# A gated recurrence and a mixing layer on one core: ordering v by DMA, a new work order, and thirteen unread matmuls

## The chip, the cores and the metric
One core of one Trainium2 chip runs the whole program. It has five engines with queues of their own: TensorE (PE, with its weight loads shown as PEld), VectorE (DVE), ScalarE (ACT), GpSimd (POOL) and SyncE (SP), and sixteen DMA engines that all of them share. The metric is device time in microseconds (us) of one execution.

## The reference
For four batches and eight heads, 768 tokens with 48 channels each, a state of 48 x 48 decays and is added to, token by token. The result, 384 wide, goes through a layer that mixes over tokens and channels.

```python
for t in range(S):
    cur = einsum('bhd,bhe->bhde', u * k[t], v[t])
    y[t] = einsum('bhd,bhde->bhe', r[t], state + cur)
    state = w[:, :, None] * state + einsum('bhd,bhe->bhde', k[t], v[t])
x = y.transpose(0, 2, 1, 3).reshape(B, S, H * D)
theta = x @ w_theta
yy = einsum('ts,bsd->btd', w_tok_r, x * cos(theta)) + einsum('ts,bsd->btd', w_tok_i, x * sin(theta))
u_ = x + yy
out = u_ + maximum(u_ @ w_ch, 0)
```

## The kernel before
The recurrence is computed in chunks of 128 tokens, two chunks at a time. Two chunks are called a *pair* here; there are twelve, numbered 0 to 11, three to a batch. For one pair the steps are these.

- **Loads** (lines 505 and 511, on SP). k, r and v come into a ring of nine buffers (`ld`). r is always loaded *paired*: a partition gets two tokens that follow each other, so that a run in memory is 384 bytes long, and one DMA brings 384 KB. k and v are loaded paired only for the pairs in `TWO` (pairs 0 to 3); for the others one chunk at a time, with runs of 192 bytes and 192 KB in one DMA (line 511).
- **Decays** (line 675, DVE or POOL): k and r times tables of powers of w, giving `Kw` and `Rw` in bf16. **Flips** (line 565): PE transposes them in blocks of 128 x 128 into a PSUM bank; line 576 (ACT) or 574 (DVE) copies the bank out as `KT` and `RT`.
- **Scores** (line 714): KT times RT for each chunk, 128 x 128 per head, masked on DVE into `mAT` (line 720). **PD and diag** (lines 727, 736): KT times RT elementwise, summed with u by small matmuls, copied by ACT as `dg` (line 741), and multiplied with v as `yd` (line 744).
- **Outer** (lines 759 and 773): sums of k times v for the state, kept by small steps (`N`, `T`, `Sb`) on DVE, POOL and ACT. **Outputs** (lines 833, 842): state times RT, and mAT times v (`vb`), then x on DVE (line 850).
- **Theta** (line 865), sine and cosine on ACT (lines 870, 873), and z = x times both on DVE (line 876).

The mixing of a batch needs z of its three pairs. For each of its six output chunks, twelve matmuls of 384 columns (line 896) run over WrT and WiT, then `un` on DVE (903), a transpose by DMA (585) or by PE, three matmuls with W_ch (919), and `fin` on DVE (923), which is stored by SP (929). In all there are 288 mixing matmuls. The weights come in bf16 by eight casting DMAs from POOL (line 524), six of them for the token weights, which PE then flips.

**v.** outer wants v in the order in which k was loaded, and outputs wants it in token order. For a paired load the two differ. The cast `v2` (line 628) keeps the paired order and is read by outer2 (line 773). For token order, `put` (line 639) multiplies v2 by a 0/1 matrix, `place`, that POOL fills at the start (lines 434, 435): two matmuls of 384 columns for each chunk. `put out` (line 647 on ACT, 649 on DVE) copies the bank into `vb`. vb is read by outputs and by yd.

**The order of the work.** Nothing runs in the order in which the code names it. Each step is added to a plan with an engine, an assumed duration, what it reads and writes, and the PSUM banks it needs. `RANK` gives each step its priority and `MOVED` the steps that go to their second engine; both lists were found by a search outside the program. `Plan.order` then plays the plan through with its assumed durations, banks and DMA queues, and emits the instructions in the order in which the plan would start them. So each engine's queue is fixed when the program is built, and an engine does not pass a waiting instruction. Steps with `port` (decays, PD, yd, z and others on DVE and POOL) are kept from running on both engines at once.

**Completion semaphores.** The framework gives the DMAs that SP and ACT issue eight completion semaphores, in turn, in the order in which the program names the DMAs. A DMA that takes a semaphore has a wait in front of it, on its issuing engine, until the DMA that had the semaphore before has landed. In the kernel before, all such DMAs are SP's.

**Start.** `stuff` is filled, and twelve steps `warm` are in the plan with 427 ns each, but emit nothing (`range(0)`). Log w is spread over the partitions by two fp32 matmuls (line 428), and a small flip of w and u follows (line 446), copied on DVE (line 450).

Of the kernel before, what the change touches and what calls it, by code (L numbers as in the profile page):

```python
# [18 lines left out]
BF16 = mybir.dt.bfloat16  # L19
# [15 lines left out]
class Plan:  # L35
# [50 lines left out]
    def order(self):  # L86
# [23 lines left out]
        while times or dma_next < math.inf:  # L110
# [26 lines left out]
            for e in engines:  # L137
# [23 lines left out]
                if t.xfer:  # L161
                    q = int(e == POOL)
                    queues[q].append(t)
                    if len(queues[q]) == 1:
                        todo[q] = t.xfer + ns
                else:
                    t.end = done + LAT[e]
# [17 lines left out]
TWO = (0, 1, 2, 3)  # L185
W_BY_DMA = ()
WARM = 12
# [45 lines left out]
    61, 102, 105, 107, 112, 120, 140, 143, 155, 165, 173, 176, 185, 206, 222, 235, 238, 247,  # L233
    255, 267, 290, 377, 378, 390, 409, 412, 421, 441, 453, 542, 573, 593, 605, 615, 702,
# [18 lines left out]
def kernel(  # L253
# [49 lines left out]
    place = sb.tile([C, 2, 2, C], BF16, name="place")  # L303
# [12 lines left out]
    v2s = ring(len(TWO), [C, H, 2, D], BF16, "v2")  # L316
# [38 lines left out]
    def setup():  # L355
# [15 lines left out]
        def stuff_fill():  # L371
            nc.vector.memset(stuff, 1.0)
            nc.vector.memset(stuff.rearrange("p (a b) -> p a b", b=2)[:, :, 1], -0.5)
        P.add(DVE, 250, stuff_fill, wr=["stuff"], prio=-102)
        for i in range(WARM):
            def warm_up(i=i):
                for _ in range(0):
                    nc.tensor.matmul(bank(("warm", i))[:, :2 * C], stuff[:, :C], stuff,
                                     start=True, stop=True)
            P.add(PE, 427, warm_up, rd=["stuff"], acq=[("warm", i)], prio=-92, name="warm")  # L380

# [51 lines left out]
        def placing():  # L433
            nc.gpsimd.memset(place, 0.0)
            nc.gpsimd.affine_select(
                out=place, in_=place, compare_op=Alu.not_equal, fill=1.0, base=0,
                channel_multiplier=-2, pattern=[[C, 2], [-1, 2], [1, C]])
        P.add(POOL, 1200, placing, wr=["place"], prio=-94)

# [3 lines left out]
        P.add(SP, 800, wu_load, wr=["wu"], prio=-90 + 0.0055, xfer=300)  # L443
# [546 lines left out]
```

## Time and profile before

| | us |
|---|---|
| median of three runs (lowest, highest) | 143.91 (141.71, 144.53) |
| the profiled execution | 140.77 |
| its span, first to last instruction | 139.1 |
| PE busy | 124.2 (89%) |
| DVE busy | 107.8 (77%) |
| ACT busy | 75.8 (55%) |
| POOL busy | 73.5 (53%) |

In the lines of the profile, L896 is line 896 of the kernel. The slices divide the span into forty equal parts, and a digit is the busy share in tenths. Matmuls are pipelined: a busy time counts each from its start to its modelled end, so two that follow each other overlap, and the distance of their starts (the pitch) is the better measure of what one costs. "SPq" is SP's instruction stream with its DMA issues.

### The profile page before, as it was taken

The numbers are of one execution on the slowest core, as the hardware profiler recorded it, in microseconds if no ns is written. First come the engines' busy times: TensorE is split into PE (matmuls) and PEld (weight loads), VectorE is DVE, ScalarE is ACT, GpSimd is POOL, SyncE is SP. The second block draws the span as 40 slices with busy tenths as digits, with TensorE's granted clock in tenths as the row PEclk, the third lists the DMA queues.
The fourth block names the chain that finished last, engine by engine and source line by source line (L and its number), as shares of the span: only waits on it lengthen the run. The fifth ranks groups of instructions, "written<-read, shape, count | busy, mean of one in ns | idle before, by whom it ended". The sixth has DMA issues, their size and how long they took to land.

```text
span 139.1 us, 4098 instructions
## 1 busy us (share of the span) xinstructions
PE 124.2 (89%) x1677; PEld 84.6 (61%) x1677; DVE 107.8 (77%) x200; ACT 75.8 (55%) x142; POOL 73.5 (53%) x60
## 2 busy tenths in 40 slices
PE   2389876999999999999999989999799999999980
PEld 2168655876777666677657657675455665656640
DVE  6189989797897799989799889988689665526381
ACT  7969985899965634789413767339751305000010
POOL 6027989994055594996687899499640000000000
PEclk9999999599999999999999999999999999999996
DMA  2899999999989989999997998999862023255644
GB/s 61 230 323 321 308 222 202 195 244 210 207 174 220 194 169 226 152 209 185 158 223 133 233 255 179 223 147 232 169 232 51 7 57 66 106 167 61 170 176 163
DMA packets 72637, 25.24 MB, mean 182 GB/s; under 512 B 67241, under 2 KB 72618, under 8 KB 72618
## 3 DMA queue, kind: packets, MB, share of 16 engines
q1 hardware_dynamic: 70186, 22.03, 77.2%
q0 software_dynamic: 2432, 2.95, 12.2%
q8 instruction: 13, 0.21, 0.6%
q14 instruction: 6, 0.05, 0.2%
HBM read 20.06 MB, written 4.72 MB: 178 GB/s over the span
## 4 chain that ended last, share of the span: by engine, by line
PE 47%; DMA 16%; POOL 13%; DVE 12%; issue 6%; ACT 3%; SPq 0%; POOLq 0%; DVEq 0%; ACTq 0%
PE bank L896 23%; PE bank L919 7%; DMA fin_all<-in_moe_w_tok_r_dram 6%; PE bank L565 6%; POOL PD L727 5%; DMA ld<-in_k_dram 4%; PE bank L865 4%; POOL Rw L675 3%; DMA uu_all<-uu_all 3%; DVE mAT L720 3%; DMA ld<-in_r_dram 3%; POOL yd L744 2%; POOL Kw L675 2%; DVE fin_all L923 2%; ACT KT L576 1%
## 5 line engine op out<-in xcount | busy, mean ns | idle before, releaser
L896 PE MATMUL bank<-z,WrT 128*128 128x384 bf16 x144 | 46.8, 326 | 0.1
L896 PE MATMUL bank<-z,WiT 128*128 128x384 bf16 x144 | 46.8, 326 | 0.0
L720 DVE TENSOR_TENSOR mAT<-bank,mask 128x512 bf16<-128x512 f32 x48 | 30.9, 681 | 2.1 <-PE bank L714 2.0
L727 POOL TENSOR_TENSOR PD<-RT,KT 128x1024 bf16<-128x1024 bf16 x10 | 21.2, 2123 | 2.2 <-DVE z L876 1.1
L675 POOL TENSOR_TENSOR Kw<-ld,kpow 128x768 bf16<-128x768 f32 x7 | 12.7, 1811 | 16.7 <-DVE z L876 8.5
L870 ACT ACTIVATE trig<-bank,pi 128x384 f16<-128x384 f32 x24 | 13.7, 599 | 12.1 <-issue 4.5
L923 DVE SCALAR_TENSOR_TENSOR fin_all<-bank,uu_all 128x384 f32<-128x384 f32 x24 | 12.9, 553 | 9.1 <-PE bank L919 8.9
L896 PEld LDWEIGHTS <-WrT 128*128 128x128 bf16 x144 | 14.1, 98 | 8.4
L896 PEld LDWEIGHTS <-WiT 128*128 128x128 bf16 x144 | 14.1, 98 | 8.3 <-issue 0.2
L903 DVE TENSOR_TENSOR uu_all<-bank,x 128x384 bf16<-128x384 f32 x24 | 13.1, 552 | 6.0 <-PE bank L896 5.3
L744 POOL TENSOR_TENSOR yd<-dg,vb 128x768 bf16<-128x768 f32 x10 | 14.7, 1472 | 3.1 <-ACT dg L741 1.8
L675 POOL TENSOR_TENSOR Rw<-ld,rpow 128x768 bf16<-128x768 f32 x8 | 14.5, 1813 | 2.3 <-PE bank L565 1.4
L919 PE MATMUL bank<-Wch,uu_all 128*128 128x384 bf16 x72 | 14.3, 326 | 1.3 <-DMA uu_all<-uu_all 0.9
L576 ACT ACTIVATE KT<-bank 128x1024 bf16<-128x1024 bf16 (+1 forms) x11 | 10.8, 981 | 8.5 <-PE bank L565 7.3
L865 PE MATMUL bank<-Wth,xT 128*128 128x384 bf16 x72 | 14.5, 326 | 0.0
L576 ACT ACTIVATE RT<-bank 128x1024 bf16<-128x1024 bf16 (+1 forms) x12 | 11.8, 986 | 3.8 <-PE bank L565 3.8
L850 DVE TENSOR_TENSOR x<-bank,yd 128x384 bf16<-128x384 f32 x24 | 12.4, 548 | 1.7 <-issue 0.9
L876 DVE TENSOR_TENSOR z<-x,trig 128x1536 bf16<-128x1536 bf16 x12 | 12.1, 1009 | 0.8 <-ACT trig L873 0.8
L873 ACT ACTIVATE trig<-bank 128x384 f16<-128x384 f32 x24 | 11.9, 512 | 0.0
L565 PE MATMUL bank<-ident,Rw 128*128 128x128 bf16 x96 | 8.1, 230 | 2.5 <-DVE Rw L675 2.4
L919 PEld LDWEIGHTS <-uu_all 128*128 128x128 bf16 x72 | 6.6, 98 | 5.8 <-DMA uu_all<-uu_all 1.3
L576 ACT ACTIVATE uu_all<-bank 128x384 bf16<-128x384 bf16 x1 | 0.5, 490 | 16.7 <-PE bank L565 16.7
(105 smaller groups left out, 190.5 us busy)
## 6 DMA issues: line engine op xcount, KB each, us to landing
ld<-in_r_dram SPq DMA_DIRECT2D x12, 384.0 KB, 4.8
out_dram<-fin_all SPq DMA_DIRECT2D x11, 384.0 KB, 2.8
ld<-in_k_dram SPq DMA_DIRECT2D x16, 192.0 KB, 4.9
ld<-in_v_dram SPq DMA_DIRECT2D x16, 192.0 KB, 5.6
ld<-in_k_dram SPq DMA_DIRECT2D x4, 384.0 KB, 4.9
ld<-in_v_dram SPq DMA_DIRECT2D x4, 384.0 KB, 5.8
x<-in_moe_w_tok_i_dram POOLq DMA_DIRECT2D x1, 384.0 KB, 6.2
z<-in_moe_w_tok_r_dram POOLq DMA_DIRECT2D x1, 384.0 KB, 7.6
```

The source lines that it names most:

```text
L565: nc.tensor.matmul(bank16(tok)[:, i * C:(i + 1) * C], s, ident, is_transpose=True, start=(i == 0), stop=(i == n - 1))
L576: nc.scalar.activation(dst, src, Act.Copy)
L675: eng.tensor_mul(X[:, :, hs, :D], src[:, :, hs], pw[:, :, hs])
L720: P.add(DVE, dve_ns(HP * C), lambda hi=hi, tk=tk, mAT=mAT: nc.vector.tensor_mul(mAT[:, hi], bank(tk[hi]).rearrange("p (h t) -> p h t", h=H ...
L727: eng.tensor_mul(PD, RT, KT)
L744: eng.tensor_mul(yd.rearrange("p a h d -> p (a h) d"), wide(dg, D), vb.rearrange("p a h d -> p (a h) d"))
L865: nc.tensor.matmul(bank(th)[:, :HD], xT[:, t, dk, :], Wth[:, dk, :], start=(dk == 0), stop=(dk == ND - 1))
L870: P.add(ACT, act_ns(HD, False) + 65 + (1300 if g == 0 and t == 0 else 0), lambda th=th, t=t, trig=trig: nc.scalar.activation(trig[:, t, 0] ...
L896: nc.tensor.matmul(bank(tm)[:, :HD], (WrT, WiT)[ri][:, so, to * C:(to + 1) * C], z[:, so, ri], start=(part == 0 and i == 0), stop=(part == ...
L903: P.add(DVE, dve_ns(HD), lambda tm=tm, t=t, to=to, un=un: nc.vector.tensor_add(un[:, t], bank(tm)[:, :HD], x[:, to]), use=[tm], rd=[("x", ...
L919: nc.tensor.matmul(bank(tf)[:, :HD], uT[:, t, dk, :], Wch[:, dk, :], start=(dk == 0), stop=(dk == ND - 1))
L923: nc.vector.scalar_tensor_tensor(fin[:, t], bank(tf)[:, :HD], 0.0, un[:, t], op0=Alu.max, op1=Alu.add),
```

## The change
Five things change.

1. Put, put out and `place` go. In their place `order` issues four DMAs from ACT's queue for each paired v: for each chunk and each of the two interleaved halves, 64 rows of 768 bytes go from v2 to every second row of vb, from SBUF to SBUF. v2 is laid out so that a row is contiguous, and has four buffers.
2. Pair 4 joins `TWO`: its k and v are loaded paired.
3. Thirteen matmuls of 256 columns are emitted right behind the second spread, into the bank that the plan uses last. Nothing reads them. The empty `warm` steps go, and the flip of w and u now stands behind the spreads.
4. Some assumed durations in the plan change, and an ACT step may have a latency (a negative `xfer`).
5. `RANK` and `MOVED` are new, so that every engine's order is new, and some steps change engine. By count, five more PD are on DVE and five fewer on POOL; DVE has two more decays of k, one fewer of r, and two more casts of vb, and POOL takes two more yd.

```diff
-TWO = (0, 1, 2, 3)
+TWO = (0, 1, 2, 3, 4)
...
-    v2s = ring(len(TWO), [C, H, 2, D], BF16, "v2")
+    NV2 = 4
+    v2s = ring(NV2, [C, 2, H, D], BF16, "v2")
...
-        P.add(PE, 300, wu_flip, rd=["wu", "ident_f"], acq=["wu"], prio=-90)
+        P.add(PE, 300, wu_flip, rd=["wu", "ident_f", ("lw", 1)], acq=["wu"], prio=-90)
...
-                def put(tv=tv, c=c, v2=v2):
+            def order_v(vb=vb, v2=v2):
+                for c in range(2):
                     for j in range(2):
-                        nc.tensor.matmul(bank(tv)[:, :HD], place[:, c, j, :], v2[:, :, j, :],
-                                         start=(j == 0), stop=(j == 1))
...
-                P.add(ACT, act_ns(HD, False), lambda f=put_out: f(nc.scalar), use=[tv],
-                      wr=[kv[c]], prio=base + 10 * pr + 1, name="put out",
-                      alt=(DVE, dve_ns(HD), False, lambda f=put_out: f(nc.vector)))
+                        nc.scalar.dma_start(
+                            out=vb[j::2, c].rearrange("p h d -> p (h d)"),
+                            in_=v2[c * Dp:(c + 1) * Dp, j].rearrange("p h d -> p (h d)"))
+            P.add(ACT, 1100, order_v, rd=[("v2", i2)], wr=kv, prio=base + 10 * pr + 1,
+                  xfer=-2500, name="order")
...
-                P.add(PE, 330, scores, rd=kKT + kRT, wr=[("mAT", mi, hi) for hi in range(2)], acq=tk, prio=pb + 2, mode=1,
+                P.add(PE, 240, scores, rd=kKT + kRT, wr=[("mAT", mi, hi) for hi in range(2)], acq=tk, prio=pb + 2, mode=1,
...
-            ns = (210 if last else 430) if two else (110 if last else 310)
+            ns = (300 if last else 620) if two else (150 if last else 400)
...
+        spreads += t.name == "spread"
+        if t.name == "spread" and spreads == 2:
+            for _ in range(13):
+                nc.tensor.matmul(spare[:, :2 * C], stuff[:, :C], stuff, start=True, stop=True)
```

In the built program the eight-semaphore rule now joins SP's loads and ACT's order DMAs. The four order DMAs of pair 4 follow, on their semaphores, the second v half of pair 5, the first k half of pair 6, the r load of pair 6 and the first v half of pair 6; two of pair 2's follow the k and the r load of pair 3; and SP's loads of pairs 3 to 6 follow order DMAs of pairs 0 to 3 in the same way. Behind pair 4's order DMAs on ACT stand the dg copy of pair 4, KT of pair 5, an Sb and RT of pair 5.

More of the change, by code (lines that the diff above doesn't have):

```diff
@@ L160, in order @@
                 out.append(t)
-                if t.xfer:
+                if t.xfer > 0:
                     q = int(e == POOL)
@@ L166, in order @@
                 else:
-                    t.end = done + LAT[e]
+                    t.end = done + LAT[e] - min(t.xfer, 0.0)
                     for b in t.uses:
@@ L184 @@
 U_BY_DMA = tuple(range(11))
-TWO = (0, 1, 2, 3)
+TWO = (0, 1, 2, 3, 4)
 W_BY_DMA = ()
-WARM = 12
 V_CAST = ()
@@ L191 @@
 RANK = [
[38 rows of a table removed]
[37 rows of a table added]
 ]
 MOVED = [
-    61, 102, 105, 107, 112, 120, 140, 143, 155, 165, 173, 176, 185, 206, 222, 235, 238, 247,
-    255, 267, 290, 377, 378, 390, 409, 412, 421, 441, 453, 542, 573, 593, 605, 615, 702,
+    64, 67, 77, 79, 84, 89, 120, 150, 195, 208, 213, 220, 230, 231, 240, 261, 273, 350, 384,
+    414, 496, 502, 515, 520, 534, 566, 578, 588, 675,
 ]
@@ L302 @@
     gate = sb.tile([1, 1], F32, name="gate")
-    place = sb.tile([C, 2, 2, C], BF16, name="place")
     rpow = sb.tile([C, 2, H, D], F32, name="rpow")
@@ L369, in setup @@
               wr=["warm"], prio=-99)
[L371 to L380, printed above, removed]
         def tok():
@@ L431, in setup @@
                   use=[] if s == 0 else ["lw"], wr=[("lw", s)], prio=-98 + s, name="spread")
[L433 to L438, printed above, removed]
         def wu_load():
@@ L442, in wu_load @@
             nc.sync.dma_start(out=wu[HP:, :, :D], in_=u.rearrange("(a b) d -> a b d", b=2))
-        P.add(SP, 800, wu_load, wr=["wu"], prio=-90 + 0.0055, xfer=300)
+        P.add(SP, 800, wu_load, wr=["wu"], prio=-90 + 0.0055, xfer=900)
         def wu_flip():
@@ L620, in front @@
                 continue
-            i2 = g % len(v2s)
+            i2 = g % NV2
             v2 = v2s[i2]
@@ L625, in cast2 @@
                     "p (h q) -> p h q", h=H)[:, :, :2 * D]
-                dst = v2.rearrange("p h j d -> p h (j d)")
+                src = src.rearrange("p h (j d) -> p j h d", j=2)
+                dst = v2
                 if eng is nc.scalar:
@@ L633, in front @@
                   alt=(POOL, pool_ns(2 * HD) - 200, True, lambda f=cast2: f(nc.gpsimd)))
-            for c in range(2):
-                tv = ("V", g, c)
-                def put(tv=tv, c=c, v2=v2):
+            def order_v(vb=vb, v2=v2):
+                for c in range(2):
                     for j in range(2):
-                        nc.tensor.matmul(bank(tv)[:, :HD], place[:, c, j, :], v2[:, :, j, :],
-                                         start=(j == 0), stop=(j == 1))
-                P.add(PE, 340, put, rd=[("v2", i2), "place"], wr=[kv[c]], acq=[tv],
-                      prio=base + 10 * pr + 1, name="put")
-                def put_out(eng, tv=tv, c=c, vb=vb):
-                    src = bank(tv)[:, :HD].rearrange("p (h d) -> p h d", h=H)
-                    if eng is nc.scalar:
-                        eng.activation(vb[:, c], src, Act.Copy)
-                    else:
-                        eng.tensor_copy(vb[:, c], src)
-                P.add(ACT, act_ns(HD, False), lambda f=put_out: f(nc.scalar), use=[tv],
-                      wr=[kv[c]], prio=base + 10 * pr + 1, name="put out",
-                      alt=(DVE, dve_ns(HD), False, lambda f=put_out: f(nc.vector)))
+                        nc.scalar.dma_start(
[3 more added lines that the diff above has]
+                  xfer=-2500, name="order")
         prev = None
@@ L764, in outer, with outer2 @@
                                     skip_group_check=True)
-            def outer2(ts=ts, Kw=Kw, v2=v2s[g % len(v2s)], sums=sums):
+            def outer2(ts=ts, Kw=Kw, v2=v2s[g % NV2], sums=sums):
                 for i, cs in enumerate(sums):
@@ L774, in outer2 @@
                                     bank(ts)[hi * Dp:(hi + 1) * Dp, o:o + D],
-                                    Kw[:n, j, 2 * hp + hi, :], v2[:n, 2 * hp + hi, j, :],
+                                    Kw[:n, j, 2 * hp + hi, :], v2[:n, j, 2 * hp + hi, :],
                                     start=(i == 0 and hp == 0 and j == 0),
@@ L778, in outer2 @@
                                     skip_group_check=True)
-            ns = (210 if last else 430) if two else (110 if last else 310)
-            P.add(PE, ns, outer2 if two else outer, rd=kK + ([("v2", g % len(v2s))] if two
+            ns = (300 if last else 620) if two else (150 if last else 400)
+            P.add(PE, ns, outer2 if two else outer, rd=kK + ([("v2", g % NV2)] if two
                   else kv), acq=[ts], prio=pb + 2, mode=2, name="outer")
@@ L947 @@
     order = P.order()
+    first = {}
+    for t in order:
+        for b in t.acq:
+            first.setdefault(P.bank_of[b], t.start)
+    spare = bank_t[max(range(P.nbanks), key=lambda i: first.get(i, math.inf))]
+    nc.vector.memset(stuff, 1.0)
+    nc.vector.memset(stuff.rearrange("p (a b) -> p a b", b=2)[:, :, 1], -0.5)
+    spreads = 0
     made, before = nc.cur_bb.bb.instructions, None
```

75 rows, old and new, of the table RANK are left out of this document.

## Prediction
> **What bounds the kernel now.** I read the page's forty slices first, then busy time in windows, then the chain of waits, then SP's timeline.
>
> ```profile
> PE   2389876999999999999999989999799999999980
> ...
> DMA  2899999999989989999997998999862023255644
> ```
>
> ```profile
> 7.65:35.00 27.35, 24.32 (x461) 19.00 (x462) 24.04 (x42) 23.34 (x43) 21.95 (x19) 0.94 1.17 251
> 35.00:70.00 35.00, 34.92 (x524) 24.12 (x523) 30.98 (x51) 22.87 (x42) 21.91 (x13) 1.00 1.11 191
> 70.00:105.00 35.00, 33.08 (x476) 22.12 (x473) 30.83 (x55) 19.42 (x36) 27.32 (x17) 1.00 1.06 202
> ```
>
> The columns are stretch, length, then busy us of PE, weight loads, DVE, ACT, POOL, then granted clock, DMA share, GB/s. From 35 us on PE is never short of work for long, so every us by which PE is stopped there is a us of the span. The DMA engines are busy the whole way to 100 us. Before 35 us several engines are near full together and PE is not the only bound.
>
> The chain of waits, in order of time, shows what releases the first mixing matmuls (L896):
>
> ```profile
> 26.38 8.45 DMA fin_all<-in_moe_w_tok_r_dram
> 34.82 0.05 issue
> 34.87 0.84 PE bank L565 x12
> 35.71 0.97 PE bank L865 x6
> 36.69 0.65 PE bank L896 x4
> ```
>
> From 36.69 to the end of the last L919 (135.4) PE takes 98.7 us. At the pitches of the chain (mixing, theta, chan 0.1625 us a matmul, flips 0.056, scores 0.034, small ones 0.02 to 0.04) the matmuls ordered there sum to 94.6 us; 4.1 us are idle and loss. The tail after it (last evacuation, store, barrier) is 139.1 - 135.4 = 3.7 us.
>
> SP's timeline, with the us an issue took in the second column:
>
> ```profile
> 18.96 6.44 SPq L505 DMA_DIRECT2D ld<-in_r_dram  x1
> 25.49 4.29 SPq L511 DMA_DIRECT2D ld<-in_v_dram  x2
> ...
> 29.87 9.78 SPq L511 DMA_DIRECT2D ld<-in_k_dram  x2
> ...
> 44.89 1.06 SPq L505 DMA_DIRECT2D ld<-in_r_dram  x1
> 46.04 3.50 SPq L511 DMA_DIRECT2D ld<-in_v_dram  x2
> ```
>
> The loads of pairs 4 and 5 crawl while POOL's eight weight casts run (16 to 40 us); the list of DMA issues for 18 to 24 us gives the r load of pair 4 16.4 us to landing. The loads of pair 6 are issued only at 42.87 to 47, and land about 5 us later.
>
> **What goes, at its rows.** The sixteen put matmuls (L639) ran at 326 to 527 ns of latency, but by start times the first four took 0.33 us each and the rest 0.163: 4 x 0.33 + 12 x 0.163 = 3.3 us of PE. All but four lie before 20 us, where PE also idles (3.3 of 5 us busy at 20 to 25 us), so only part of it is worth time. Pair 4 becomes paired: 32 small matmuls for 24, +0.2 us PE. Eight put-outs go: 7 x 0.513 on ACT, 0.55 on DVE. The 0/1 matrix: 1.2 us of POOL at 2.0 to 3.2 us, where POOL next waits 6.3 us for a load: nothing. Two loads of 384 KB replace four of 192 KB, at about 1.15 us each in the queue: -2.3 us of SP and DMA.
>
> **The 13 unread matmuls.** They stand behind the spreads, which end at 4.41 us, and ahead of the flip of w and u. At the half-rate pitch of the early rows (0.33 us for 384 columns, so 0.22 for 256) they take 2.8 us and end at 7.2; PE's first useful flip starts at 7.65. They fit that gap. The flip of w and u moves from 5.0 to about 7.2, and its copy on DVE (L450), now second in DVE's decay work, holds the decay of Rw behind it from 7.03 to about 7.6: cost 0 to 0.6 us, I take 0.5. The gain: PE's pitch was half of the later one from 7.65 to about 11 us, 3.3 us of work at double length, so 0 to 1.6 us, 0.66 of which is in the puts already counted. Nothing in the trace shows an earlier start of the full pitch, so both ends stay; I take 1.0. All of it lies ahead of the first mixing matmul, which the weights decide (below), so in the sum it is hidden; it counts only in rival (a).
> The Trainium skill (TensorE: Matmul & The Clock Gate, Part 1) says that the array starts at half rate and is released after some 3.4 us of sustained activity, on a free-running window. By that rule spreads and unread matmuls together (2.8 to 7.2 us) would release it before or soon after 7.65, and the whole 1.6 us would come. The trace agrees in that 7.65 + 3.4 is where the pitch changes, though the granted-clock row shows 1.00 from the start; no run here shows the rest.
>
> **The order by DMA.** Twenty DMAs of 64 rows x 768 B, issued by ACT. No ACT-issued DMA is in the trace. One issue: below by nothing, above by the 1.15 us of SP's issues into a full queue; nearest are SP's shortest (0.37 to 0.53 us), I take 0.42: 8.4 us of ACT, 5.0 of it (three pairs) before 23 us, where ACT is 90% busy. Landing: between the 2.8 us of the output stores and the 16.4 of the load above; nearest is the SBUF-to-SBUF transpose with 3.1, longer while weights run. The 0.98 MB cost about 3 us of DMA at the 325 GB/s of the early loads, against the 2.3 saved.
>
> **The search.** Counting each form in both instruction orders and pricing it by its row: POOL -11.5 us (five PD at 2.12, two Kw at 1.81 go; two yd, one Rw come), DVE +5.0 (five PD at 0.68, two Kw at 0.95, two vb at 1.58 come; two yd at 1.82 go), ACT -6.9 before its 8.4 of issues. DVE is 88% busy at 35 to 105 us; POOL's relief meets no PE wait above 0.8 us in total. I take 0, with -1.5 to +2.5 for what an order of this kind can do to the 4.1 us of idle above.
> Up to the first mixing matmul the weights still decide: in the new order POOL issues three casts behind pair 0's yd (about 18.5 us) and the next behind pair 1's yd, which needs pair 1's dg; that stands on ACT behind eight order DMAs. ACT's work to there, start to start from its rows: the first v2 cast starts at 9.5, behind two half-size evacuations, and takes 0.75; four issues; two full evacuations, two kpow, w256, dg, two v2 casts and two Sb, 5.25; eight issues; RT, KT and dg, 2.0: 17.5 + 12 x 0.42 = 22.5 us; yd, two cast issues (0.8 each) and the 7 to 8 us of landing give 33 to 34, flips and theta 1.6: first mixing at about 35 (34 to 38). So about 1.7 us ahead of 36.69.
>
> **Where it is lost again.** DMAs of SP and ACT share eight completion semaphores, taken in program order, and a DMA waits until the one eight before has landed. In the new order the four order DMAs of pair 4 wait for pair 5's last v half, pair 6's first k half, **pair 6's r load and pair 6's first v half**: prefetches issued just ahead in the program. Before, SP ran behind: it issued pair 6's r load at 44.89, in program order before the vb cast of pair 4, which ACT did at 43.39. When do they land now? In units of 1.15 us, the program before needed 26 loads to that v half, landing 46.04 + 5.6 = 51.6; now it is 24, so -2.3, + about 2.5 for sixteen order DMAs, and the weights start 1 to 2 us later while SP's pair 4 loads wait for pair 1's order DMAs: 50 to 53; ACT would be there at 42 to 45. I take the last landing as 50.5.
> Queued on ACT behind these waits: the dg copy of pair 4, KT of pair 5, Sb, RT. PE waits for the dg copy: scores take the same PSUM bank. From the first mixing matmul to those scores PE has 40 mixing matmuls 6.5, 40 flips 2.25, 16 scores 0.55, 32 outer 0.7, 8 diag 0.3 = 10.3 us; 84.4 remain behind. So PE stops at 35 + 10.3 = 45.3 to 46 and goes on at 50.5 + 0.42 issue + 0.2 copy = 51.1.
> Sum: 51.1 + 84.4 + 4.1 + 3.7 = **143.3 us span**, before 139.1 (check of the method with before: 36.7 + 94.6 + 4.1 + 3.7 = 139.1). The profiled execution took 140.77, 1.67 more than its span: 145.0, a ratio of 1.030. The median of the runs shown, 143.91, is 2.2% above the profiled execution; on that scale 148.2. I give **146.5**, between the two.
>
> **Rivals.**
> (a) *Faster: the prefetches land before ACT asks.* For: the last loads of a batch are free to go as soon as slots and semaphores are, two loads fewer stand ahead, and a load outside the weights' time lands in 4.8 us. Then nothing stops PE: puts -2.4 (part at 20 us idle is lost already), clock -1.6, first mixing at about 33: 139.1 - 4.0 = 135 span, 136.8, on the median scale 139.8. It decides when the last landing comes before 44 us. Against it: DMA share above 1.0 in every window to 50 us. Chance 0.28.
> (b) *Within 2%.* The landing comes at 44.5 to 49, so ACT's wait eats the early gain: 137 to 141.7, as a time 138.6 to 143.4. Also here: the unread matmuls lift no clock and the order is free. Chance 0.24.
> (c) The forecast, 0.48. Inside it, a worse end: PE idles over 4 us at 46 to 51. After the idle stretch at 19 to 23 us the clock row stood at 0.50 from about 24.5 to 27.7; the same again costs 1.7 us, and landings at 53 another 2.5: 147.5 span, 149 to 152.
>
> Range: from between (a)'s two scales (136.8 and 139.8) to near the upper of (c)'s worse end: 138 to 151.5. A measurement of this kernel tells about 2% from no change (its runs spread over 2%). Faster 0.28, same 0.24, slower 0.48.
>
> **What would show it.** PE's pitch for 128-column flips at 7.5 to 11 us: 0.056 if the clock came. ACT with a gap of 5 us or more at 42 to 51 us, in front of or inside the order DMAs of pair 4, and PE idle at 45 to 51 released by dg. First mixing matmul at 34 to 38. If ACT has no such gap, the step of the landing is wrong and (a) holds; if PE's losses lie after 60 us, the search is to blame, and DVE will be the releaser.

## The result, and the profile after

The changed kernel took 149.18 us (median of four runs, 148.81 to 150.27), the kernel before 142.81 (140.59 to 144.53) on the same chip: a ratio of 1.058 with a 95% interval of 1.046 to 1.070. Two of the four executions of the kernel before (143.91 and 144.53) ran in a slower state that some executions of one and the same kernel show, and the ratio compares the other two (141.71 and 140.59) with the changed kernel's four. It is 5.8% slower, where the forecast's 146.5 us was 1.8% above its 143.91. The profiled execution took 150.27 us, its span is 148.6 (139.1 before). It was the longest of the four: the spans of the other three are 147.1 to 147.6, so that differences of spans below can be up to 1.5 us too large.

The forty slices of the changed kernel, as before:

```profile
PE   2959793995999905999999999999999999999990
...
PEclk9995868579999995699999999999999999999998
...
DMA  3999799999997998998999999996551125251635
```

PE has two holes that the kernel before doesn't have: slice 7 (22.3 to 26.0 us) and, empty, slice 15 (52.0 to 55.7); a lesser one is in slice 10. Behind slices 7 and 15, and at 11 us (slice 4), the granted clock is low.

The chain of waits, in order of time (start, length, what):

```profile
17.20 5.83 DMA vb<-v
23.05 11.45 DMA ld<-in_k_dram
34.52 0.97 DVE Kw L645
35.54 0.97 PE bank L545 x14
...
41.77 2.60 PE bank L866 x16
...
50.22 6.41 DMA ld<-in_v_dram
```

Before, this stretch of the chain ran through a weight load. Now it runs through an order DMA of pair 1, a k load of SP that waited for it, the decay of that k (pair 4), its flips, which PE has ahead of the last weight flips, and so to the first mixing matmul (L866), at 41.6 us in place of 36.5 (by the first start of L896; the row of the chain in the prediction begins one matmul later). Farther on the chain goes through a v load of pair 6, a prefetch that no work needs at 50 us.

What waits for it is seen in ACT's timeline (start, length, engine and line, what; in brackets the idle time ahead and what ended it):

```profile
17.86 4.90 ACTq L618 DMA_DIRECT2D vb<-v  x6
22.86 1.02 ACT L556 ACTIVATE RT<-bank 128x1024 bf16<-128x1024 bf16 x1 [4.74 <-DMA vb<-v]
...
47.49 0.86 ACT L609 ACTIVATE v<-ld 128x768 bf16<-128x768 f32 x1
50.79 6.34 ACTq L618 DMA_DIRECT2D vb<-v  x4
57.26 0.18 ACT L711 ACTIVATE dg<-bank 128x16 f32<-128x16 f32 x1 [8.91 <-DMA vb<-v]
```

ACT has cast v of pair 4 at 48.35, issues the first order DMA at 50.79, the last from 56.66 to 57.13, and only then copies dg. The first two rows explain the hole in slice 7: with eight order DMAs of pairs 1 and 2 issued one behind the other up to 22.8, ACT copies RT at 22.86 and KT at 23.78, and PE waits 2.9 us for that KT. Here is SP's timeline, as shown of before:

```profile
23.05 0.37 SPq L485 DMA_DIRECT2D ld<-in_k_dram  x1
...
29.75 13.19 SPq L491 DMA_DIRECT2D ld<-in_k_dram  x2
43.04 2.13 SPq L485 DMA_DIRECT2D ld<-in_r_dram  x1
...
49.04 1.09 SPq L485 DMA_DIRECT2D ld<-in_r_dram  x1
50.22 3.55 SPq L491 DMA_DIRECT2D ld<-in_v_dram  x2
```

The first v half of pair 6 is issued at 50.22 and lands 6.41 us later, at 56.6: it is the load whose completion semaphore the last order DMA of pair 4 takes, and ACT goes on with that landing. Before, SP issued it at 46.04. SP's own loads wait for order DMAs as well: its three waits for them end at 14.35 and 15.30 (pair 3's k and r, behind pair 0's) and at 23.05 (pair 4's k, behind pair 1's). The waits view of PE, ACT and SP (who waits for whom: us in total, times, longest):

```profile
PE bank L684 <- ACT dg L711: 5.2, 1, 5.2
PE bank L684 <- ACT KT L556: 2.9, 1, 2.9
...
ACT dg L711 <- DMA vb<-v: 8.9, 1, 8.9
...
SPq L485 <- DMA vb<-v: 9.4, 3, 6.1
```

### The profile page after: what moved, and what is told of

Read it like the earlier page. It is cut to its first block, busy times and chain, and to the rows that moved or that the text cites. A ratio compares the mean times of both kernels' runs of the same rounds, so it can differ in the third digit from the quotient of the medians.

```text
span 148.6 us, 4133 instructions
## 1 busy us (share of the span) xinstructions
PE 128.4 (86%) x1682; PEld 88.2 (59%) x1682; DVE 107.3 (72%) x209; ACT 69.2 (47%) x130; POOL 62.2 (42%) x53
## 4 chain that ended last, share of the span: by engine, by line
PE 56%; DMA 16%; ACT 8%; POOL 6%; DVE 4%; issue 4%; ACTq 2%; SPq 1%; POOLq 0%
PE bank L866 27%; DMA ld<-in_k_dram 8%; PE bank L545 6%; PE bank L889 6%; PE bank L835 5%; DMA ld<-in_v_dram 4%; DMA vb<-v 4%; POOL PD L697 3%; PE bank L812 3%; PE bank L684 2%; PE bank L933 2%; ACTq L618 2%; ACT RT L556 1%; ACT KT L556 1%; POOL Kw L645 1%
## 5 line engine op out<-in xcount | busy, mean ns | idle before, releaser
L866 PE MATMUL bank<-z,WrT 128*128 128x384 bf16 x144 | 47.2, 329 | 0.0
L866 PE MATMUL bank<-z,WiT 128*128 128x384 bf16 x144 | 47.2, 329 | 0.0
L714 POOL TENSOR_TENSOR yd<-dg,vb 128x768 bf16<-128x768 f32 x12 | 17.7, 1473 | 21.8 <-ACT RT L556 7.8
L873 DVE TENSOR_TENSOR uu_all<-bank,x 128x384 bf16<-128x384 f32 x24 | 13.2, 552 | 10.6 <-PE bank L866 10.2
L645 POOL TENSOR_TENSOR Rw<-ld,rpow 128x768 bf16<-128x768 f32 x9 | 16.4, 1818 | 7.2 <-DVE Kw L645 4.7
L866 PEld LDWEIGHTS <-WrT 128*128 128x128 bf16 x144 | 14.2, 98 | 8.4 <-issue 0.2
L866 PEld LDWEIGHTS <-WiT 128*128 128x128 bf16 x144 | 14.2, 98 | 8.1 <-issue 0.2
L684 PE MATMUL bank<-RT,KT 64*128 64x128 bf16 x192 | 10.2, 239 | 8.6 <-ACT dg L711 5.2
L556 ACT ACTIVATE KT<-bank 128x1024 bf16<-128x1024 bf16 (+1 forms) x10 | 9.8, 981 | 12.2 <-PE bank L545 11.9
L835 PE MATMUL bank<-Wth,xT 128*128 128x384 bf16 x72 | 15.1, 342 | 0.3 <-ACT xT L556 0.3
L645 POOL TENSOR_TENSOR Kw<-ld,kpow 128x768 bf16<-128x768 f32 x5 | 9.1, 1818 | 15.1 <-DVE uw L456 12.5
L889 PE MATMUL bank<-Wch,uu_all 128*128 128x384 bf16 x72 | 14.8, 326 | 0.1
L684 PEld LDWEIGHTS <-KT 64*128 64x128 bf16 x192 | 6.3, 102 | 12.4 <-issue 8.7
L697 POOL TENSOR_TENSOR PD<-RT,KT 128x1024 bf16<-128x1024 bf16 x5 | 10.6, 2123 | 4.0 <-ACT RT L556 4.0
L645 DVE TENSOR_TENSOR Kw<-ld,kpow 128x768 bf16<-128x768 f32 (+1 forms) x8 | 6.9, 861 | 4.3 <-DMA ld<-in_k_dram 2.5
```

The lines of the kernel that those rows point to most:

```text
L556: nc.scalar.activation(dst, src, Act.Copy)
L645: eng.tensor_mul(X[:, :, hs, :D], src[:, :, hs], pw[:, :, hs])
L684: nc.tensor.matmul(bank(tk[hi])[:, hp * C:(hp + 1) * C], KT[q, hp, c, :], RT[q, hp, c, :], start=(hp == 0), stop=(hp == HP - 1))
L697: eng.tensor_mul(PD, RT, KT)
L714: eng.tensor_mul(yd.rearrange("p a h d -> p (a h) d"), wide(dg, D), vb.rearrange("p a h d -> p (a h) d"))
L835: nc.tensor.matmul(bank(th)[:, :HD], xT[:, t, dk, :], Wth[:, dk, :], start=(dk == 0), stop=(dk == ND - 1))
```

## The experiments

The theory after the result: the time went into two waits for completion semaphores, SP's loads behind the order DMAs of pairs 0 and 1, and ACT's order DMAs of pair 4 behind SP's prefetches. The rivals: the new order of the work itself; the DMA engines being too full for these rows whichever queue issues them; the unread matmuls and the clock.

### Order DMAs replaced by copies

```diff
+                if g in (4,):            # or (0, 1, 2, 3), or TWO
+                    nc.scalar.activation(vb, v2, Act.Copy)
+                    return
                 for c in range(2):
                     for j in range(2):
                         nc.scalar.dma_start(
```

> The changed kernel, with pair 4's four order DMAs replaced by one ACT copy of v2 into vb (0.85 us at the row of the v cast). Left out: the token order of pair 4's v. Theory (PE's stop at 52.2 to 57.5 us is ACT waiting for the semaphores of pair 6's prefetches): dg of pair 4 is there before PE's scores, PE does not stop, first mixing matmul still at 41.6; 41.6 + 10.3 + 84.4 + 2.8 to 4.1 + 3.7 = 142.8 to 144.1 us of span, less up to 1.7 for half-rate matmuls behind the stop: 141 to 144, against 148.6. Rival (the new order of the work is at fault, and the wait only covers it): PE stops near 52 us for DVE or ACT all the same, span 146 to 149.

> The changed kernel, with the order DMAs of pairs 0 to 3 replaced by one ACT copy each; pair 4 keeps its four. Left out: the token order of v in pairs 0 to 3. Theory (SP's loads of pair 4 stand behind the order DMAs' semaphores, and this moves the first mixing matmul from 36.7 to 41.6 us): SP issues pair 4's k load at about 17 instead of 23 us, first mixing matmul at 36 to 38; SP then reaches pair 6's r load at about 45, its v half lands at 51 to 53, so PE stops from 47 to 52: span 143 to 145. Rival (the weights or DVE's extra work set the first mixing matmul): it stays at 40 to 42, span 147 to 149.

> The changed kernel, with all twenty order DMAs replaced by five ACT copies; unread matmuls, the paired pair 4 and the new order of the work stay. Left out: the token order of v in the paired pairs. Theory (all of the loss is in the two waits for DMA semaphores): first mixing matmul at 36 to 38, no stop of PE at dg; 37 + 10.3 + 84.4 + 3.5 + 3.7 = 139, so 137 to 141 us of span, level with the kernel before (139.1). Rival (the new order itself costs several us): over 142.

Measured. copy_pair4: span 143.7, and PE has no stop at dg; the first mixing matmul is at 43.3, so the saving is that of the second wait alone. Its times spread from 142.54 to 147.36, so no size is read from it; pair4_by_pool, below, tests the same wait with times that agree. copy_pairs0to3: span 143.8, ratio 1.027 (1.019 to 1.036), first mixing at 38.3. copy_all: span 138.6, ratio 0.992 (0.989 to 0.996), first mixing at 38.6 and no stop. The spans of the three profiled executions lie in the theories' ranges. The first mixing matmuls do not: 43.3 where 41.6 was expected, 38.3 and 38.6 where it was 36 to 38. In copy_all what follows takes 100.0 us in place of the kernel before's 102.6. So the new order of the work, the paired pair 4 and the unread matmuls, together with the dropped puts, are no loss: all of the loss is in the twenty DMAs. copy_pairs0to3 gains 4.7 us by the medians, all twenty together 9.5.

SP's and ACT's timelines in copy_pairs0to3 show the second wait by itself:

```profile
45.55 2.26 SPq L491 DMA_DIRECT2D ld<-in_v_dram  x2
```

```profile
45.04 6.80 ACTq L621 DMA_DIRECT2D vb<-v  x4
51.96 0.18 ACT L714 ACTIVATE dg<-bank 128x16 f32<-128x16 f32 x1 [6.95 <-DMA vb<-v]
```

SP, no longer held by order DMAs, issues pair 6's v halves from 45.55, the first lands at 51.3, ACT issues the last order DMA at 51.37 and copies dg at 51.96. PE goes on at 52.20.

### The same DMAs with other semaphores

```diff
+                queue = nc.gpsimd if g in (4,) else nc.scalar
                 for c in range(2):
                     for j in range(2):
-                        nc.scalar.dma_start(
+                        queue.dma_start(
```

> The changed kernel with one difference: pair 4's four order DMAs are issued from POOL's queue, whose DMAs have completion semaphores of their own, in place of ACT's. The same bytes are moved between the same buffers at the same place of the work. Theory (PE's stop at 52 us is made by the semaphores that ACT's order DMAs share with SP's prefetches, not by moving v by DMA): ACT copies dg of pair 4 at 47 to 51, PE does not stop for it, span 141 to 145 against 148.6, as with pair 4 copied (143.7). POOL pays four issues of about 0.8 us (the row of the cast issues) ahead of its decays of pair 5. Rival 1 (the DMA engines are too full at 47 to 57 us for these rows, whichever queue issues them): vb of pair 4 lands at 56 or later, PE stops in outputs or yd instead, span 147 to 149. Rival 2 (POOL's issues hold its decays, and PE waits for Kw or Rw of pair 5): 145 to 148.

Measured: 145.17 us against 149.18, span 143.4, ratio 1.031 (1.025 to 1.037). POOL's timeline, and ACT's copy of dg in the same run:

```profile
47.07 2.16 POOL L619 DMA_DIRECT2D vb<-v  x4 [0.23 <-issue]
49.24 1.83 POOL L646 TENSOR_TENSOR Kw<-ld,kpow 128x768 bf16<-128x768 f32 x1
...
54.11 1.87 POOL L715 TENSOR_TENSOR yd<-dg,vb 128x768 bf16<-128x768 f32 x1 [0.82 <-DMA vb<-v]
```

```profile
48.19 0.18 ACT L712 ACTIVATE dg<-bank 128x16 f32<-128x16 f32 x1 [1.41 <-PE bank L707]
```

Four issues took POOL 2.16 us, and nothing held them; dg is copied at 48.19, released by PE and no longer by a DMA. The first is issued at 47.07, and yd, which needs all four, waits for the last of them to 54.1. This run settles the point that the copies could not: the bytes, the buffers and the place in the work are those of the changed kernel, only the queue and with it the semaphores differ, and PE's 5.2 us at dg are gone. That it is the semaphores and not something else in ACT's queue rests on the landings: in the changed kernel ACT's last order DMA starts at 56.66, as that v half lands (56.63), and in copy_pairs0to3 at 51.37, as it lands there; at 10.36, with the DMA engines full as well (share 1.17), ACT issued four in 2.48 us. Rival 1 falls; of rival 2 a little is true (PE waits 1.7 us for Kw from POOL).

The Trainium skill (DMA: Bandwidth & Descriptors, Rules for kernel authors) says that spreading DMAs over SP, ACT and GpSimd doesn't help bandwidth and only saves the sequencers' issue time. Here moving four DMAs saved 4.0 us by the medians, by a third thing: which DMAs an issue must wait for.

### Fewer and larger order DMAs

```diff
-                    for j in range(2):
-                        nc.scalar.dma_start(
-                            out=vb[j::2, c].rearrange("p h d -> p (h d)"),
-                            in_=v2[c * Dp:(c + 1) * Dp, j].rearrange("p h d -> p (h d)"))
+                    nc.scalar.dma_start(out=vb[:, c], in_=v2[c * Dp:(c + 1) * Dp])
```

> The changed kernel with two order DMAs for each pair instead of four (one for each chunk, 64 partitions x 1536 B read, 128 rows of 768 B written): same bytes, half the issues and half the semaphores. Pair 4's two then follow pair 5's first v half and pair 6's first k half; SP's pair 4 loads follow fewer order DMAs. Theory (issues and shared semaphores cost the time, not the bytes): first mixing matmul at 37 to 40, PE's stop at dg 0 to 2 us, span 139 to 144. Rival (the bytes, moved row by row beside the weights, are what is slow): span 146 to 149.

Measured: span 141.9, ratio 1.024 (1.015 to 1.033), first mixing at 38.2, stop at dg 0.6 us. SP waits 1.8 us for order DMAs in place of 9.4 and issues pair 6's first v half at 46.92 in place of 50.22, with the same bytes moved. There are fewer issues, too, so this run alone doesn't part issues from semaphores. PE also waits for vb (0.85) and for a PD that POOL starts late behind a yd that waits for vb (1.4). The list of DMA issues of the changed kernel and of this run (count, KB each, median us to landing):

```profile
vb<-v ACTq DMA_DIRECT2D x20, 48.0 KB, 5.0
```

```profile
vb<-v ACTq DMA_DIRECT2D x10, 96.0 KB, 4.8
```

Twice the bytes land in the same time, and an issue costs ACT about the same 0.62 us (1.23 for two, 2.48 for four in the changed kernel). The Trainium skill (DMA: Bandwidth & Descriptors, Rules for kernel authors) says that below 64 KB one pays mostly overhead. These rows fit that, but loads kept the DMA engines full, and how much of the 5 us was queueing no run shows.

### The order DMAs alone, in the kernel before

```diff
                 def put(tv=tv, c=c, v2=v2):
-                    for j in range(2):
-                        nc.tensor.matmul(bank(tv)[:, :HD], place[:, c, j, :], v2[:, :, j, :],
-                                         start=(j == 0), stop=(j == 1))
+                    return
...
                 def put_out(eng, tv=tv, c=c, vb=vb, v2=v2):
+                    for j in range(2):
+                        nc.scalar.dma_start(
+                            out=vb[j::2, c].rearrange("p h d -> p (h d)"),
+                            in_=v2[c * Dp:(c + 1) * Dp, j].rearrange("p h d -> p (h d)"))
```

> The kernel before with the order DMAs alone: put emits nothing, put out issues two order DMAs from ACT for its chunk, v2 is laid out by rows; pair 4 unpaired, old order of the work, no unread matmuls. Theory (the order DMAs hold ACT and, by their semaphores, SP's loads of pairs 3 and 4, in any order of the work): ACT idle behind order DMAs by 2 to 6 us before 30 us, first mixing at 37.5 to 41, span 139.5 to 144. Rival (only the new order brings DMAs and loads into each other's way): 3.3 us of put matmuls and 4 us of ACT are gained, span 136 to 139.

Measured: span 151.2, ratio 1.083 (1.078 to 1.088), first mixing at 40.5. Worse than the theory's range of spans, by a second stop that it did not count; and the waits of ACT that it expected before 30 us came at 33 to 45. PE's timeline:

```profile
42.18 0.50 PE L840 MATMUL bank<-vb,mAT 128*128 128x48 bf16 x8
48.81 0.48 PE L840 MATMUL bank<-vb,mAT 128*128 128x48 bf16 x8 [6.13 <-DMA vb<-v]
```

Here it is pair 3 whose outputs stop PE: two of its order DMAs are issued at 33.35, the other two only at 43.67, each held on ACT by a load of SP (ACT's idle times of 3.5 and 5.3 us at 37 and 45 us end with a landing of `ld<-in_k_dram`). So the mechanism needs neither the new order nor the paired pair 4; with the order DMAs in it the old order is the slower one (1.083 against 1.058).

### The unread matmuls and the clock

In the changed kernel `range(13)` becomes `range(0)`; in the kernel before, thirteen are emitted behind the second spread as in the changed kernel.

> The changed kernel without the thirteen unread matmuls. In the changed kernel the full rate was there from 7.4 to about 10.9 us and gone again after PE's 1.3 us wait for the v cast. Theory (what the unread matmuls win is lost at that wait, and lies ahead of a first mixing matmul that other things decide): span 147.5 to 149.5 against 148.6. Rival 1 (they are worth the 1.6 us that a half-rate start costs): 150 to 151. Rival 2 (they only shift the full rate to where it is of no use, and cost clock after 11 us, where the kernel before had full rate to 23 us): clock row near 1.00 from 11 to 20 us, span 145 to 147.5.

> The kernel before, with thirteen unread matmuls of 256 columns behind the two spreads and ahead of the flip of w and u; nothing else. Theory: PE's pitch is full from about 7.4 us, but the weights decide the first mixing matmul at 36.7 us: span 138.5 to 140, ratio 0.995 to 1.005 to the kernel before. Rival 1 (the early part is on the path): 1.6 us less, ratio 0.985 to 0.99. Rival 2 (the clock, raised early, drops again between 9 and 20 us): half pitch there, first mixing at 37 to 39, ratio 1.00 to 1.015.

Measured. no_unread: 148.75 us, ratio 1.053 (1.046 to 1.060) to the kernel before, the changed kernel's 1.058 within the intervals; span 147.0. The clock row is at 1.00 from 11 to 15 and 0.70 from 15 to 20 us, but it can't be taken at its word ahead of the first change that it shows (below): by the pitch PE ran at half rate to about 15 us, at full rate to 18 and at half again, not as rival 2 had it. The first mixing matmul is at 38.4, but PE then stops 6.3 us for dg in place of 5.2 and goes on at 55.6 in place of 57.5, when pair 6's v half, issued at 49.05, has landed. So most of the 3.2 us is eaten at the second wait. The spans of its four executions, 146.3 to 147.4, lie in rival 2's range and not in the theory's, but against the changed kernel's 147.1 to 148.6 no difference is shown. (The first mixing matmul alone is no sharp measure: pair4_by_pool and copy_pair4, whose programs are the changed kernel's up to there, have it at 40.0 and 43.3.) before_13_unread: ratio 1.005 (1.002 to 1.009), first mixing at 36.7. The theory's time holds, its picture only in part. The clock row is at 1.00 from 7 to 20 us, but it stands there in the kernel before as well while the pitch is halved, so the pitch must tell: the flips at 7.50 still ran at half rate (four in 0.61 us, as in the kernel before), and the first faster group is the puts at 9.19 (four in 0.87 us against 1.39). In the changed kernel the flips at 8.23 were fast (four in 0.40 us; 0.61 in no_unread). So the full rate came 1 to 2 us earlier in before_13_unread, and won nothing; where the half per cent comes from stays open.

The rate didn't stay in the changed kernel: windows of its early part (stretch, length, busy us of PE, weight loads, DVE, ACT, POOL, then granted clock, DMA share, GB/s):

```profile
8.20:9.10 0.90, 0.80 (x8) 0.53 (x9) 0.44 (x1) 0.90 (x4) 0.00 (x0) 1.00 1.17 318
9.10:10.40 1.30, 0.01 (x2) 0.04 (x3) 1.27 (x2) 1.23 (x3) 0.00 (x0) 1.00 1.17 322
10.40:11.40 1.00, 1.00 (x35) 0.91 (x35) 1.00 (x3) 0.00 (x0) 0.00 (x0) 0.78 1.17 325
11.40:12.40 1.00, 1.00 (x12) 1.00 (x11) 0.62 (x1) 0.00 (x0) 0.00 (x0) 0.50 1.17 325
```

PE waits 1.29 us for the v cast on ACT, and about half a microsecond after it went on the clock falls to 0.50. In the other profiles with unread matmuls in the changed kernel that had the full rate by then it was lost between 10 and 13 us as well; that the pause is the cause is not shown. Below are order_two_dmas and then two_dmas_pair4_pool, which have the same program up to 45 us, each with a window and with groups of eight flips.

```profile
15.00:20.00 5.00, 4.79 (x87) 4.09 (x88) 4.94 (x11) 2.54 (x6) 5.00 (x5) 0.50 1.12 306
17.28 1.03 PE L545 MATMUL bank<-ident,Kw 128*128 128x128 bf16 x8
```

```profile
15.00:20.00 5.00, 4.80 (x98) 4.07 (x96) 4.94 (x10) 3.11 (x9) 4.95 (x4) 1.00 1.00 267
17.85 1.03 PE L545 MATMUL bank<-ident,Kw 128*128 128x128 bf16 x8
30.54 0.61 PE L545 MATMUL bank<-ident,Kw 128*128 128x128 bf16 x8
```

The clock rows say 0.50 and 1.00, but the flips took the same 1.03 us, where eight at full rate take 0.61. So the second ran at half rate too, from 7.4 to about 22 us, and its row, at 1.00 from the start, doesn't show it. Where a row shows a fall, as behind the pause above, the pitch agrees (eight flips at 11.19 us took 1.03). By the pitch the first had the full rate at 8.3 us, lost it at about 11.5 and had it again at 28; the second had it from about 22 on. Their first mixing matmuls are at 38.2 and 38.4 us, so in these two it made no difference when the full rate came. The Trainium skill (TensorE: Matmul & The Clock Gate, Part 1) says that the window over which activity is judged runs freely, so that the same kernel changes rate at different points from run to run; these two agree. It puts the fall back to half rate behind an idle window of about 3.4 us. The pause here was 1.3 us, so the fall came without such a window.

### Versions meant to be better

Three kinds were tried on top of the two DMAs a pair. In the first, pair 4 is loaded by halves as in the kernel before, so that its v needs no ordering:

```diff
-TWO = (0, 1, 2, 3, 4)
+TWO = (0, 1, 2, 3)
...
+                if g == 4:
+                    P.add(ACT, 1, lambda: None, rd=kv, prio=base + 10 * pr + 1, name="none")
```

> Two order DMAs for each of pairs 0 to 3, and pair 4 loaded one chunk at a time as in the kernel before, so that its v needs no ordering; order of the work as in the changed kernel. Theory (with pair 4's semaphore wait gone and few order DMAs ahead of SP's pair 4 loads, what is left is the better order behind the first mixing matmul, 100.0 us there in the run with five copies against 102.4 in the kernel before): first mixing at 37.5 to 39, span 138 to 140.5, level with the kernel before. Rival (two loads more and the waits of yd and outputs for vb cost what the order wins): 140.5 to 143.

> As the run before in this list, without the unread matmuls. Theory (they are worth nothing here): the same span within 1 us. Rival 1: 1.6 us more. Rival 2 (they cost clock between 11 and 28 us, where the run with two order DMAs stood at 0.50 to 0.63): 1 to 3 us less, and a first mixing matmul at 36 to 37.

Measured: 1.077 (1.069 to 1.085) and 1.063 (1.052 to 1.074), spans 150.9 and 149.7, though the first mixing matmul of the first is at 37.4. These two don't test what they were meant to. The edit changes the assumed durations, the plan played through differently, and every engine's order came out anew; PE then waits for transposes (2.9 us for those of `uu_all`, 1.3 for one of x) and masks (2.7). They show what the given order is worth: some 10 us between two orders of the same work. So the same unpairing was done with the plan's steps left alone:

```diff
+                if g == 4:
+                    src, dst = Ls[iv][:, :, :, :D], vb
...
             def order_v(vb=vb, v2=v2, g=g):
+                if g == 4:
+                    return
```

> Two order DMAs for pairs 0 to 3; k and v of pair 4 are loaded by halves and its v is cast straight into token order, but the plan is played with the changed kernel's own steps and durations, so that the order on every engine stays that of the changed kernel (in the run unpaired4_two_dmas the plan came out differently: DVE's order alone differs in over a hundred rows). Theory (pair 4's semaphore wait is what order_two_dmas still loses behind the first mixing matmul): first mixing at 38 to 38.8, 100 to 101 us behind it as in the run with five copies, span 138 to 139.8. Rival (two loads more make SP's prefetches late, or the loss lies elsewhere): 140.5 to 143.

Measured: 143.04 us, ratio 1.012 (1.007 to 1.017), span 141.3, first mixing at 37.7. PE doesn't stop for dg, but the span is the rival's: 103.6 us behind the first mixing matmul, with PE waits for a transpose by DMA (1.5), for Wth (1.2, ahead of it) and for POOL's decays. Without the unread matmuls:

> pair4_plain_two_dmas without the unread matmuls: the version meant to beat both kernels. Theory (the two effects add): span 136.5 to 138.5, ratio 0.98 to 0.995 to the kernel before. Rival (the clock gained ahead of the first mixing matmul is hidden by the weights): the same as pair4_plain_two_dmas within 0.7 us.

Measured: the times spread from 142.45 to 147.37, ratio 1.015 (1.008 to 1.022); nothing finer is read from it; the theory's 0.98 to 0.995 is excluded. order_two_dmas without the unread matmuls:

> order_two_dmas without the unread matmuls. Theory (with them the full rate comes early, is lost at PE's wait for the v cast and stays away to 28 us; without them it comes at about 11 us and stays): clock row at or near 1.00 from 11 to 20 us, first mixing at 36.5 to 38.2, span 140 to 141.9 against 141.9. Rival (they are worth a half-rate start): 142.5 to 143.5.

Measured: ratio 1.025 (1.018 to 1.033), with the unread matmuls 1.024: no difference. The profiled span, 141.8, is at the theory's upper end with first mixing at 37.7, but two other executions have 142.5 and 143.4, in the rival's range, and by the pitch the full rate was there only from about 15 to 18 us (eight flips took 1.03 us at 10.65, 0.62 at 16.44 and 1.04 at 18.03). So the part of the theory on the clock failed, and the rival is neither shown nor excluded. Last, pair 4's two DMAs from POOL:

> Two order DMAs for each pair, pair 4's two from POOL's queue. Theory: of order_two_dmas (141.9) the waits of dg, vb and PD for pair 4's order DMAs go, 2 to 3 us: span 138.8 to 140.5, ratio 0.995 to 1.01 to the kernel before. Rival (POOL's two issues ahead of its decays cost what ACT gains): 141 to 143.

Measured: 142.78 us, ratio 1.014 (1.008 to 1.019), span 141.2. dg is copied at 46.6 and no wait for an order DMA holds PE, yet the span lies with the rival: PE waits for POOL's decays (0.8 and 0.6), for Wth and for a transpose. Without the unread matmuls:

> As the run before in this list, without the unread matmuls. Theory (they bring the full rate early and lose it at PE's wait for the v cast; their sum is nothing that can be measured): the same ratio within 0.01. Rival: 0.01 or more lower, for the clock between 11 and 17 us.

Measured: 1.020 (1.012 to 1.027), no difference that the intervals show; the rival falls.

No version that orders v beat the kernel before. copy_all, which leaves the ordering out, is 0.8% ahead of it. No run shows more than that from the new order, the paired pair 4 and the dropped puts.

## Why the prediction was right and wrong

The forecast's sum against the profile:

| | forecast | measured |
|---|---|---|
| first mixing matmul | 35 | 41.6 |
| PE reaches pair 4's scores | 45.3 to 46 | 52.0 |
| last landing that ACT waits for | 50.5 | 56.6 |
| PE goes on | 51.1 | 57.5 |
| from there to the end (84.4 + 4.1 + 3.7) | 92.2 | 91.1 |
| span | 143.3 | 148.6 |

- **The mechanism was right.** PE stops at pair 4's scores for the dg copy, which stands on ACT behind four order DMAs, which wait for pair 6's prefetches; the 10.3 us of PE work from the first mixing matmul to that point came out at 10.4. pair4_by_pool shows that it is the queue's semaphores.
- **The step that failed is the landing**, "I take the last landing as 50.5": it was 56.6, and all of the 5.3 us by which the span was missed comes from there (6.4 at PE's going on, less 1.1 behind it). The forecast had the landing one microsecond ahead of the kernel before's 51.6. Its own terms, 2.3 us saved on loads against 2.5 for the bytes of the order DMAs, give 51.8; the 50.5, near the lower end of its 50 to 53, has no reason beside it. SP was 4.2 us behind (50.22 against 46.04), and the landing took 6.4 in place of 5.6. The order DMAs were priced as bytes in the DMA engines. What they cost SP was waiting: 9.4 us in three waits, of which the forecast counted 1 to 2 at most. copy_pairs0to3 shows it: with sixteen of the twenty gone SP issues that v at 45.55, PE goes on at 52.20, and the span is 143.8, close to the forecast's 143.3. That run moves fewer bytes, too; order_two_dmas, with all of them and 1.8 us of such waits, still issues that v at 46.92. So some 3.3 of the 4.2 us are not the bytes.
- **The step from the span to the time.** 143.3 against 139.1 is 3.0%, and on the scale of the profiled executions the sum is 145.0 (150.27 measured). The 146.5 lies between that and a second scale resting on 143.91, and against 143.91 it stands for 1.8% only.
- **First mixing at 35 (34 to 38)** failed too, and for the same reason: "so the weights decide" left out that SP's pair 4 loads, which the text itself named as waiting for pair 1's order DMAs, feed flips that PE has queued ahead of the mixing. With these waits gone it is at 38.2 to 38.6, still later than forecast: the second yd that gates POOL's casts ran at 24.3 us in copy_all where 22.5 was worked out, and from 32.2 to 37.5 us the chain runs through ACT's queue (dg, xT, sine and cosine, two weight copies, xT), which the forecast had at 1.6 us with the flips. This miss cost little by itself, since PE would have stopped at 45 instead of 52 and still waited for the landing: in no_unread the first mixing matmul came 3.2 us earlier and PE went on 1.9 us earlier, 1.2 of it because SP issued that v earlier.
- **Issue and landing of an order DMA.** 0.42 and 3.1 us were taken, 0.62 and 5.0 measured, the first within its bounds of 0 to 1.15, the second between 2.8 and 16.4. Twenty issues cost ACT 4 us more than taken. Eight of them stand ahead of the KT in slice 7; the chain ran through SP's k load there, and what that hole cost by itself is not shown.
- **The unread matmuls**: 13 at 0.22 us, ending at 7.2, and hidden, as worked out: nothing is won. The flips at 8.23 us had the full pitch, so the clock came, as it did by 9.2 us in before_13_unread. But in two_dmas_pair4_pool the same matmuls brought no full rate before 22 us, with PE busy 96 to 100% from 11 us on, so release after some 3.4 us of activity, which the prediction cites, is no rule to count on here. That the full rate would be lost again at 10.9 us was not foreseen, and doesn't matter.
- **The search: effect 0 (-1.5 to +2.5).** copy_all puts it, with the first mixing matmul 2 us later and the rest 2.6 us shorter, at about zero, together with the paired pair 4 and the dropped puts; alone it was not tested. The count behind it was half right: POOL's busy time fell by 11.3 us (11.5 forecast, though the forms that it lists sum to 9.5), but DVE's by 0.5 where +5.0 was forecast, among other things because the casts of vb took 0.55 us each and not 1.58. What follows PE's stop took 91.1 us, less than worked out, so nothing there points to it either.
- **Rival (a)**, prefetches landing before ACT asks, needed a landing before 44 us; it was over 12 us off. **The worse end of (c)** (149 to 152) was the right branch: half clock behind the stop (0.50 to 62 us) and a landing later than 53.

## What to carry to other kernels

In this program a DMA cost more than its bytes and its issue: it took a completion semaphore from a set of eight, and the engine that issued the next DMA on that semaphore stood still until the earlier one had landed. When a compute engine starts to issue DMAs, list for each what it follows on its semaphore and, as much, which loads of the old queue now follow it; price both by landings. Of the 5.8% lost here, a queue with semaphores of its own for pair 4 took away 2.7, half as many DMAs of twice the size 3.4, and both together 4.4, without moving a byte less.

## What the runs showed that was not expected

- The row of the granted clock read 1.00 while the matmuls ran at half rate: from 7.4 to 22 us in two_dmas_pair4_pool, from 7.5 to about 15 in no_unread, from 7.65 to about 10.6 in the kernel before. The pitch is what tells the rate.
- Thirteen unread matmuls up to 7.3 us brought the full rate by 8.3 us in one profile and only at about 22 us in another, of the same program to that point.
- A 48 KB and a 96 KB copy from SBUF to SBUF land alike, in 5.0 and 4.8 us, beside loads that keep the DMA engines full.
- POOL issued the four order DMAs in 2.16 us, ACT in 2.48 where nothing held it.
- Two orders of the same work, played through by the same plan from slightly different steps and durations, differ by 9.6 us of span (150.9 and 141.3).
